# w_down as one transfer over 128 partitions in place of eight over 64, in a decode kernel that streams a KV cache

## The chip, the core and the metric

The kernel runs on one core of a Trainium2 chip. The metric is the device time of one execution in microseconds (us): 2534.58 us is the median of three runs (2534.54 to 2534.76). A separate execution was taken with the hardware profiler; it gives the page, the chain of waits, the timelines and the trace that are read below.

## The reference

One token passes through two branches that are mixed by a gate:

```python
x = A_x                                          # 1 x 1 x 512
g = sigmoid((x * gate_w).sum(-1, keepdims=True))
q = (x @ wq) as 32 heads of 128
p = softmax(q . k_cache * 128 ** -0.5)           # 32 heads x 65536 keys
a = (p @ v_cache as 4096 columns) @ wo           # 4096 x 512
b = (silu(x @ w_gate) * (x @ w_up)) @ w_down     # 512 x 1792, 512 x 1792, 1792 x 512
out = g * a + (1 - g) * b
```

All inputs are bf16. The two caches have 32 x 65536 x 128 elements each and are read once. w_down is 1792 x 512, that is 1,835,008 bytes.

## The kernel before, in words

**Tiles.** A K or a V tile is 16384 rows of one head's cache: 128 partitions with 128 rows of 128 elements each, 32 KB in a partition, 4096 KB in all. There are G = 4 tiles to a head and N = 128 tiles of each kind. All of them live in one ring of five buffers (`SLOTS`, tag "big"). wq, the pair w_gate and w_up (`gu_t`), w_down (`wd_t`) and half of wo (`wo_t`) take a turn in that ring too. So a load can start only when the tile that had its buffer five allocations earlier has been read for the last time. In order, the ring holds wq, K 0, K 1, `gu_t`, `wd_t`, and then K 2 in wq's buffer, K 3 in K 0's, K 4 in K 1's, V 0 in `gu_t`'s and K 5 in `wd_t`'s.

**Work on a tile.** VectorE (DVE) multiplies a K tile by the query (L240) and halves its columns three times by additions (L244). TensorE (PE) adds up the remaining 16 columns with identity matmuls into the scores (L254). After four K tiles the softmax of a head is made (L266 to L281). A V tile takes 32 matmuls of 128x512 (L302) with the probabilities as weights.

**Order.** The order is written out by hand: `steps` (L344 to L352) pairs each K tile with a V tile that runs several tiles behind, and the loop at L355 issues, for each step, first the loads and then the work. Every load but one is issued by SyncE (SP), in program order, so a load that waits holds back all later loads. Transfers share eight completion semaphores in turn: one waits for an earlier one to land before its semaphore is used again. These waits stand at SP's instructions in the trace.

**The small branch.** `feed_forward_in` (L169) makes x @ w_gate and x @ w_up behind K tile 1. `feed_forward_mid` (L189) forms the hidden vector `hT` on VectorE, as 128 partitions by 14 columns; two matmuls with every second column of the identity (L202) spread it over 64 partitions by 28 columns, ScalarE (ACT) copies it to `h2` (L206), and 28 matmuls of 64 rows (L209) multiply it with w_down into `b_ps`. `feed_forward_out` (L218) scales it and adds it into the output's sum `a_ps` (L227).

**w_down's load.** It lies on partitions 0 to 63, 28 rows of 512 in each, 28,672 contiguous bytes per partition. `load_wd` (L142) makes one transfer of eight partitions at a time: parts 0 and 1 at L150, ahead of K tile 2, and parts 2 to 7 at L359, behind it.

**The end.** The last V tiles come in pieces (L365), then the second half of wo in five pieces (L367). After the last V matmul stand 16 projections (L406 to L410), the copy at L413 and the store at L414.

Of the kernel before, what the change touches and what calls it, by code (L numbers as in the profile page):

```python
# [8 lines left out]
ACT = mybir.ActivationFunctionType  # L9
ALU = mybir.AluOpType  # L10
AXIS = mybir.AxisListType
P = 128
# [13 lines left out]
def kernel(  # L26
# [14 lines left out]
    nc = tc.nc  # L41
    bf16 = mybir.dt.bfloat16
    f32 = mybir.dt.float32

    _, H, Sk, Dh = A_k_cache.shape
    D = A_x.shape[2]
    F = B_w_gate.shape[1]
    KT = D // P
    FT = F // P
# [7 lines left out]
    consts = ctx.enter_context(tc.tile_pool(name="consts", bufs=1))  # L57
# [7 lines left out]
    psum_m = ctx.enter_context(tc.tile_pool(name="psum_m", bufs=2, space=bass.MemoryType.PSUM))  # L65
# [3 lines left out]
    def big(name):  # L69
        return ring.tile([P, NB * Dh], bf16, name=name, tag="big")  # L70
# [12 lines left out]
    ident_b = consts.tile([P, P], bf16, name="ident_b")  # L83
# [18 lines left out]
    def load(dst, cache, n, name, cuts=(0, NB)):  # L102
        h, g = divmod(n, G)
        t = big(name)
        view = t.rearrange("p (j d) -> p j d", d=Dh)
        src = cache[0, h, g * NB * P : (g + 1) * NB * P, :].rearrange("(p j) d -> p j d", j=NB)
        for a, b in zip(cuts[:-1], cuts[1:]):
            nc.sync.dma_start(out=view[:, a:b, :], in_=src[:, a:b, :])
        dst[n] = view
# [24 lines left out]
    nc.sync.dma_start(out=wgu_sb[:, 0], in_=B_w_gate.rearrange("(p t) f -> p t f", t=KT))  # L134
    nc.sync.dma_start(out=wgu_sb[:, 1], in_=B_w_up.rearrange("(p t) f -> p t f", t=KT))
    wd_t = big("wd_t")
    HP = P // 2
    GT = F // HP
    wd_sb = wd_t[:HP, : GT * D].rearrange("p (t n) -> p t n", t=GT)
    wd_rows = B_w_down.rearrange("(p t) n -> p t n", t=GT)  # L140

    def load_wd(*which):  # L142
        for i in which:
            lo = (0, 1, 2, 3, 32, 33, 34, 35)[i]
            part = slice(lo, lo + 29, 4)
            nc.sync.dma_start(out=wd_sb[part], in_=wd_rows[part])

    with nc.allow_non_contiguous_dma(reason="small"):
        nc.sync.dma_start(out=gwT, in_=gate_w.rearrange("(p t) -> p t", t=KT))
    load_wd(0, 1)  # L150
    WG = 4
    wo_tiles = {}

# [3 lines left out]
    def load_wo_end(cuts):  # L157
        t = big("wo_t")[:, : (H - WH) * D].rearrange("p (h n) -> p h n", n=D)
        rows = A_wo[WH * P :, :].rearrange("(h p) n -> p h n", p=P)
        for a, b in zip(cuts[:-1], cuts[1:]):  # L160
            nc.sync.dma_start(out=t[:, a:b, :], in_=rows[:, a:b, :])
        wo_end.append(t)

    def load_wo(g):
        wo_tiles[g] = wo_pool.tile([P, WG, D], bf16, name="wo_sb")
        rows = A_wo[g * WG * P : (g + 1) * WG * P, :]
        nc.sync.dma_start(out=wo_tiles[g], in_=rows.rearrange("(h p) n -> p h n", p=P))
# [21 lines left out]
    def feed_forward_mid(gu_sb, eg):  # L189
        nc.vector.tensor_scalar_add(eg, eg, 1.0)  # L190
        nc.vector.reciprocal(eg, eg)
        hprod = consts.tile([P, FT], f32, name="hprod")
        nc.vector.tensor_tensor(out=hprod, in0=gu_sb[:, :FT], in1=eg, op=ALU.mult)
        hT = consts.tile([P, FT], bf16, name="hT")
        nc.vector.tensor_tensor(out=hT, in0=hprod, in1=gu_sb[:, FT:], op=ALU.mult)
        xg = consts.tile([P, KT], f32, name="xg")
        nc.vector.tensor_tensor(out=xg, in0=xT, in1=gwT, op=ALU.mult)
        xs = consts.tile([P, 1], f32, name="xs")
        nc.vector.tensor_reduce(out=xs, in_=xg, axis=AXIS.X, op=ALU.add)
        h_ps = psum_m.tile([HP, GT], f32, name="h_ps", tag="misc")  # L200
        for r in range(2):
            nc.tensor.matmul(  # L202
                h_ps[:, r * FT : (r + 1) * FT], lhsT=ident_b[:, r::2], rhs=hT, start=True, stop=True
            )
        h2 = consts.tile([HP, GT], bf16, name="h2")
        nc.scalar.activation(out=h2, in_=h_ps, func=ACT.Copy)  # L206
        b_ps = psum_m.tile([1, D], f32, name="b_ps", tag="misc")
        for t in range(GT):
            nc.tensor.matmul(  # L209
                b_ps, lhsT=h2[:, t : t + 1], rhs=wd_sb[:, t, :], start=(t == 0), stop=(t == GT - 1)  # L210
            )
        g_ps = psum_m.tile([P, 1], f32, name="g_ps", tag="misc")
        nc.tensor.matmul(g_ps, lhsT=ones_f, rhs=xs, start=True, stop=True)
        eg2 = consts.tile([P, 1], f32, name="eg2")
        nc.scalar.activation(out=eg2, in_=g_ps, func=ACT.Exp, scale=-1.0)
        return b_ps, eg2
# [13 lines left out]
    def products(n, a=0, b=NB):  # L230

        h = n // G
        K = K_tiles[n][:, a:b, :]
        qb = q_bc[:, h * Dh : (h + 1) * Dh]
        q_rep = bass.AP(
            tensor=qb.tensor,
            offset=qb.offset,
            ap=[list(qb.ap[0]), [0, b - a], [1, Dh]],
        )
        yield nc.vector.tensor_tensor(out=K, in0=K, in1=q_rep, op=ALU.mult)  # L240
        half = Dh
        while half > WIDTH:
            half //= 2
            yield nc.vector.tensor_tensor(  # L244
                out=K[:, :, 0:half], in0=K[:, :, 0:half], in1=K[:, :, half : 2 * half],
                op=ALU.add,
            )
# [15 lines left out]
    def row_max(h):  # L263

        m = small.tile([P, 1], f32, name="m")
        nc.vector.tensor_reduce(out=m, in_=S_tiles[h], axis=AXIS.X, op=ALU.max)  # L266
        diag = small.tile([P, P], f32, name="diag")
        nc.scalar.activation(out=diag, in_=ident_f, func=ACT.Copy, scale=m)  # L268
        mT_ps = psum_m.tile([P, P], f32, name="mT_ps", tag="misc")
        nc.tensor.matmul(mT_ps, lhsT=ones_f, rhs=diag, start=True, stop=True)  # L270
        return mT_ps

    def exponentials(h, mT_ps):
        top = small.tile([P, 1], f32, name="top")
        nc.vector.tensor_reduce(out=top, in_=mT_ps, axis=AXIS.X, op=ALU.max)  # L275
        bias = small.tile([P, 1], f32, name="bias")
        nc.scalar.activation(out=bias, in_=top, func=ACT.Copy, scale=-scale)
        P_tiles[h] = ppool.tile([P, NBH], bf16, name="P_sb")
        nc.scalar.activation(  # L279
            out=P_tiles[h], in_=S_tiles[h], func=ACT.Exp, bias=bias, scale=scale,  # L280
            accum_out=rowsum[:, h : h + 1],  # L281
        )
        del S_tiles[h]
# [71 lines left out]
    for n, v in steps:  # L355
        if n is not None and n > 1:
            load(K_tiles, A_k_cache, n, "K_t")
        if n == 2:
            load_wd(2, 3, 4, 5, 6, 7)  # L359
        if n == 3:  # L360
            load_wo(0)
        if v is not None:
            if v % (WG * G) == 2 * G and v // (WG * G) + 1 < WH // WG:
                load_wo(v // (WG * G) + 1)
            load(V_tiles, A_v_cache, v, "V_t", (0, NB) if v < N - 2 else (0, 64, NB) if v < N - 1 else (0, 32, 64, 96, 112, NB))  # L365
            if v == N - 1:
                load_wo_end((0, 4, 8, 12, 14, 16))  # L367
        if n == 2:
            ff = feed_forward_mid(*ff)
        halves = (0, NB // 2)  # L370
        vector = iter(()) if n is None else products(n)
        if n == 0:
            vector = (i for a in halves for i in products(n, a, a + NB // 2))
        top_of = None
        if n is None:
            top_of = H - 1 if S_tiles else None
        elif n % G == 0 and n > 0:
            top_of = n // G - 1
            vector = (i for a in halves for i in products(n, a, a + NB // 2))
        if top_of is not None:  # L380
            next(vector, None)
            mT_ps = row_max(top_of)
            next(vector, None)
            exponentials(top_of, mT_ps)
        for _ in vector:
            pass
        if n == 1:
            ff = feed_forward_in()
        if n == 3:
            feed_forward_out(*ff)  # L390
        if tot_ps is not None:
            weight(*tot_ps)
            tot_ps = None
        if done is not None:
            head_column(done, head_copy(done))
        if v is not None:
            values(v)
        if top_of is not None:
            tot_ps = top_of, total(top_of)
        if n is not None:  # L400
            scores(n)
        if done is not None and done < WH:
            project(done)
        done = v // G if v is not None and v % G == G - 1 else None
# [40 lines left out]
```

## Time and profile before

| what | value | where |
|---|---|---|
| median of the runs shown | 2534.58 us | times |
| the profiled execution, its own time | 2534.51 us | times |
| its span | 2532.6 us | page |
| bytes read | 1087.64 MB, 429 GB/s over the span | page, part 3 |
| DMA in the main queue | 99.7% of 16 engines' span | page, part 3 |
| VectorE busy | 2175.5 us (86%) | page, part 1 |
| TensorE busy | 1742.4 us (69%) | page, part 1 |
| matmuls on w_down, 28 | 12.1 us busy, 629 ns each | page, part 5 |
| mean granted TensorE clock | 0.749 | page, cores |

The span goes from the first instruction to the last; 1.9 us of the execution's own time lie around it. The page gives each engine's busy time, a cut of the span into 40 slices, the DMA queues, the chain of waits that ended last, and the costliest groups of instructions. "<-" names what ended an engine's idle time. Beside these views the trace keeps every packet that a DMA engine moved, with its queue, start, duration and size, and a 4-byte record for each engine's completion of a transfer. It doesn't name the engine of a packet.

### The profile page before, as it was taken

The page shows a single profiled execution, that of the slowest core. Times are in us where ns is not written, and L with a number is a line of the kernel's source. Part 1 is how long each engine was busy: PE and PEld are TensorE (multiplying, and loading weights), DVE is VectorE, ACT ScalarE, POOL GpSimd, SP SyncE. Part 2 cuts the span into 40 slices and gives each one's busy share as a digit, 9 for nine tenths or more (in the row PEclk, how much of TensorE's full clock was granted, in tenths as well). Part 3 has the DMA queues.
Part 4 walks back from the last instruction along what each step waited for, and adds up shares of the span by engine and source line. Part 5 has one row for each costly group of instructions (what it writes and reads, how often), then busy time and mean ns, then how long its engine had stood idle before and what let it go on. Part 6 is the DMA issues. An engine that isn't in the chain of part 4 may idle for free.

```text
span 2532.6 us, 15260 instructions
## 1 busy us (share of the span) xinstructions
PE 1742.4 (69%) x6738; PEld 712.1 (28%) x6738; DVE 2175.5 (86%) x784; ACT 75.9 (3%) x207; POOL 0.7 (0%) x6
## 2 busy tenths in 40 slices
PE   4677666776677666676776677667666776677679
PEld 2222222222222222222222223222222232222223
DVE  7998888888888999998888888888888888888860
ACT  1000000000000000000000000000000000000000
POOL 0000000000000000000000000000000000000000
PEclk7677777777777676677777777777777777777779
DMA  9999999999999999999999999999999999999998
GB/s 415 433 433 430 433 433 433 432 430 435 432 432 434 431 433 432 432 433 433 432 434 433 432 434 433 432 432 434 432 431 434 433 430 434 434 431 433 434 432 339
DMA packets 42884, 1088.63 MB, mean 430 GB/s; under 512 B 4737, under 2 KB 8834, under 8 KB 9090
## 3 DMA queue, kind: packets, MB, share of 16 engines
q1 hardware_dynamic: 42674, 1087.66, 99.7%
q8 instruction: 53, 0.87, 0.1%
q14 instruction: 13, 0.11, 0.0%
q10 hardware_dynamic: 144, 0.00, 0.0%
HBM read 1087.64 MB, written 0.00 MB: 429 GB/s over the span
## 4 chain that ended last, share of the span: by engine, by line
DMA 68%; PE 22%; DVE 10%; issue 1%; ACT 0%; DVEq 0%; SPq 0%
DMA V_t<-in_A_v_cache_dram 61%; PE O_ps L302 20%; DMA K_t<-in_A_k_cache_dram 5%; DVE K_t L240 5%; DVE K_t L244 5%; PE S_ps L254 1%; DMA wo_t<-in_A_wo_dram 1%; DMA wq_t<-in_A_wq_dram 0%; PE qg_ps L117 0%; DVE m L266 0%; PE oh_ps L323 0%; PE a_ps L335 0%; PE a_ps L227 0%; ACT P_sb L279 0%; DVE top L275 0%
## 5 line engine op out<-in xcount | busy, mean ns | idle before, releaser
L302 PE MATMUL O_ps<-V_t,P_sb 128*4 128x512 bf16 x4096 | 1157.3, 453 | 496.8 <-DMA V_t<-in_A_v_cache_dram 494.3
L240 DVE TENSOR_TENSOR K_t<-K_t,q_bc 128x16384 bf16<-128x16384 bf16 (+1 forms) x160 | 1117.2, 6983 | 254.4 <-DMA K_t<-in_A_k_cache_dram 232.9
L244 DVE TENSOR_TENSOR K_t<-K_t 128x4096 bf16<-128x4096 bf16 (+3 forms) x480 | 1030.9, 2148 | 14.3
L302 PEld LDWEIGHTS <-P_sb 128*4 128x4 bf16 x4096 | 393.9, 97 | 1241.0 <-issue 897.5
L254 PE MATMUL S_ps<-K_t,ident_b 128*128 128x128 bf16 x2048 | 466.0, 394 | 107.0 <-DVE K_t L244 106.9
L254 PEld LDWEIGHTS <-ident_b 128*128 128x128 bf16 x2048 | 227.6, 115 | 330.0 <-issue 140.2
L323 PE MATMUL oh_ps<-ident_f,O_sb 4*128 4x1 f32 x256 | 57.9, 343 | 74.1 <-ACT O_sb L315 74.1
L323 PEld LDWEIGHTS oh_ps<-ident_f,O_sb 4*128 4x128 f32 x256 | 55.2, 314 | 83.7 <-ACT O_sb L315 78.9
L270 PE MATMUL mT_ps<-diag,ones_f 128*128 128x128 f32 x64 | 23.6, 468 | 79.8 <-ACT diag L268 79.8
L268 ACT ACTIVATE diag<-ident_f,m 128x128 f32<-128x128 f32 x32 | 12.8, 401 | 2099.3 <-DVE m L266 2099.3
L317 DVE COPY O_sb<-O_ps 4x256 f32<-4x256 f32 x1 | 0.4, 414 | 52.1 <-ACT O_sb L315 52.1
L270 PEld LDWEIGHTS mT_ps<-diag,ones_f 128*128 128x128 f32 x64 | 14.7, 285 | 95.6 <-ACT diag L268 95.6
L266 DVE TENSOR_REDUCE m<-S_ps 128x1 f32<-128x512 f32 x32 | 21.9, 683 | 7.4 <-PE S_ps L254 7.4
L315 ACT ACTIVATE O_sb<-O_ps 4x512 f32<-4x512 f32 (+1 forms) x32 | 18.1, 566 | 131.0 <-PE O_ps L302 131.0
L279 ACT ACTIVATE P_sb<-S_ps,bias 128x512 bf16<-128x512 f32 x32 | 22.0, 687 | 1.0
L117 PE MATMUL qg_ps<-wq_t,X_bc 128*128 128x512 bf16 x32 | 8.6, 436 | 13.2 <-DMA wq_t<-in_A_wq_dram 13.2
L293 DVE RECIPROCAL recip<-tot_ps 128x1 f32<-128x1 f32 x32 | 5.1, 160 | 12.2 <-PE tot_ps L288 12.2
L209 PE MATMUL b_ps<-wd_t,h 64*1 64x512 bf16 x28 | 12.1, 629 | 4.3 <-DMA K_t<-in_A_k_cache_dram 4.3
L288 PEld LDWEIGHTS tot_ps<-rowsum,ones_f 128*128 128x128 f32 x64 | 9.5, 188 | 14.0 <-issue 14.0
L288 PE MATMUL tot_ps<-rowsum,ones_f 128*128 128x1 f32 x64 | 12.2, 260 | 0.0
L330 ACT ACTIVATE oT<-oh_ps,rg 128x1 bf16<-128x1 f32 x32 | 8.4, 263 | 76.6 <-PE oh_ps L323 76.6
L227 PE MATMUL a_ps<-b_sb,ones_f 1*1 1x512 f32 x2 | 1.9, 1032 | 12.1 <-ACT b_sb L226 12.1
(42 smaller groups left out, 73.8 us busy)
## 6 DMA issues: line engine op xcount, KB each, us to landing
K_t<-in_A_k_cache_dram SPq DMA_DIRECT2D x127, 4096.0 KB, 35.3
V_t<-in_A_v_cache_dram SPq DMA_DIRECT2D x126, 4096.0 KB, 29.1
wq_t<-in_A_wq_dram SPq DMA_DIRECT2D x1, 4096.0 KB
K_t<-in_A_k_cache_dram SPq DMA_DIRECT2D x2, 2048.0 KB, 16.8
V_t<-in_A_v_cache_dram SPq DMA_DIRECT2D x2, 2048.0 KB
V_t<-in_A_v_cache_dram SPq DMA_DIRECT2D x3, 1024.0 KB, 29.4
wo_sb<-in_A_wo_dram SPq DMA_DIRECT2D x4, 512.0 KB, 17.3
gu_t<-in_B_w_gate_dram SPq DMA_DIRECT2D x1, 1792.0 KB
```

The costliest lines, as they stand in the source:

```text
L209: nc.tensor.matmul(b_ps, lhsT=h2[:, t : t + 1], rhs=wd_sb[:, t, :], start=(t == 0), stop=(t == GT - 1))
L240: yield nc.vector.tensor_tensor(out=K, in0=K, in1=q_rep, op=ALU.mult)
L244: yield nc.vector.tensor_tensor(out=K[:, :, 0:half], in0=K[:, :, 0:half], in1=K[:, :, half : 2 * half], op=ALU.add,)
L254: nc.tensor.matmul(S_tiles[h][:, g * NB : (g + 1) * NB], lhsT=ident_b, rhs=K_tiles[n][:, :, c], start=(c == 0), stop=(c == WIDTH - 1),)
L266: nc.vector.tensor_reduce(out=m, in_=S_tiles[h], axis=AXIS.X, op=ALU.max)
L268: nc.scalar.activation(out=diag, in_=ident_f, func=ACT.Copy, scale=m)
L270: nc.tensor.matmul(mT_ps, lhsT=ones_f, rhs=diag, start=True, stop=True)
L279: nc.scalar.activation(out=P_tiles[h], in_=S_tiles[h], func=ACT.Exp, bias=bias, scale=scale, accum_out=rowsum[:, h : h + 1],)
L288: nc.tensor.matmul(tot_ps, lhsT=ones_f, rhs=rowsum[:, h : h + 1], start=True, stop=True)
L302: nc.tensor.matmul(O_tiles[h], lhsT=P_tiles[h][:, g * NB + j : g * NB + j + 4], rhs=V_tiles[n][:, j : j + 4, :], start=(g == 0 and j == 0) ...
L315: nc.scalar.activation(out=O_sb[:, :cut], in_=O_ps[:, :cut], func=ACT.Copy)
L323: nc.tensor.matmul(oh_ps, lhsT=O_sb[:, c * Dh : (c + 1) * Dh], rhs=ident_f[0:4, c : c + 1], start=(c == 0), stop=(c == 3),)
```

## The change

w_down is laid out over 128 partitions, 14 rows of 512 each (14,336 contiguous bytes per partition), and loaded by one transfer that is issued behind K tile 2. The two transfers ahead of K tile 2 are gone, and so are the two spreading matmuls, their accumulator `h_ps` and ScalarE's copy to `h2`: the 14 columns of `hT` are the weights directly. 28 matmuls of 64 rows become 14 of 128 rows.

```diff
     wd_t = big("wd_t")
-    HP = P // 2
-    GT = F // HP
-    wd_sb = wd_t[:HP, : GT * D].rearrange("p (t n) -> p t n", t=GT)
-    wd_rows = B_w_down.rearrange("(p t) n -> p t n", t=GT)
-
-    def load_wd(*which):
-        for i in which:
-            lo = (0, 1, 2, 3, 32, 33, 34, 35)[i]
-            part = slice(lo, lo + 29, 4)
-            nc.sync.dma_start(out=wd_sb[part], in_=wd_rows[part])
+    wd_sb = wd_t[:, : FT * D].rearrange("p (t n) -> p t n", t=FT)
...
-    load_wd(0, 1)
...
-        h_ps = psum_m.tile([HP, GT], f32, name="h_ps", tag="misc")
-        for r in range(2):
-            nc.tensor.matmul(
-                h_ps[:, r * FT : (r + 1) * FT], lhsT=ident_b[:, r::2], rhs=hT, start=True, stop=True
-            )
-        h2 = consts.tile([HP, GT], bf16, name="h2")
-        nc.scalar.activation(out=h2, in_=h_ps, func=ACT.Copy)
         b_ps = psum_m.tile([1, D], f32, name="b_ps", tag="misc")
-        for t in range(GT):
+        for ft in range(FT):
             nc.tensor.matmul(
-                b_ps, lhsT=h2[:, t : t + 1], rhs=wd_sb[:, t, :], start=(t == 0), stop=(t == GT - 1)
+                b_ps,
+                lhsT=hT[:, ft : ft + 1],
+                rhs=wd_sb[:, ft, :],
+                start=(ft == 0),
+                stop=(ft == FT - 1),
             )
...
         if n == 2:
-            load_wd(2, 3, 4, 5, 6, 7)
+            nc.sync.dma_start(out=wd_sb, in_=B_w_down.rearrange("(p t) n -> p t n", t=FT))
```

## The prediction on record

> **What bounds the kernel.** I read the page's parts 2 and 3 first, then the chain of waits at the end, then the end's timeline. Parts 2 and 3:
>
> ```profile
> GB/s 415 433 433 430 433 433 433 432 430 435 432 432 434 431 433 432 432 433 433 432 434 433 432 434 433 432 432 434 432 431 434 433 430 434 434 431 433 434 432 339
> ...
> q1 hardware_dynamic: 42674, 1087.66, 99.7%
> q8 instruction: 53, 0.87, 0.1%
> ```
>
> The rate is flat at 430 to 435 GB/s from the second slice to the last but one, and packets occupy 99.7% of sixteen engines' time: the DMA engines bound the kernel from beginning to end, and no compute stage does. The chain at the end says what follows the last loads:
>
> ```profile
> 2472.70 31.39 DMA V_t<-in_A_v_cache_dram
> ...
> 2504.16 20.87 DMA wo_t<-in_A_wo_dram
> ...
> 2527.07 2.69 PE a_ps L335 x12
> ```
>
> and the timeline there:
>
> ```profile
> 2504.14 20.88 PE L302 MATMUL O_ps<-V_t,P_sb 128*4 128x512 bf16 x96 [1.62 <-DMA V_t<-in_A_v_cache_dram]
> ...
> 2529.79 0.68 DVE L413 CAST out_sb<-a_ps 1x512 bf16<-1x512 f32 x1 [3.85 <-PE a_ps L335]
> 2530.49 0.28 SPq L414 DMA_DIRECT2D out_dram<-out_sb  x1
> ```
>
> The 126th V tile (V 125) was issued at 2472.70 and landed at 2504.09. PE had run dry 1.62 us before, then ran 96 matmuls back to back (217 ns each), the projections and the store. So the end is V 125's landing plus 28.5 us. A transfer has landed when the last of its sixteen engines is done, so the question is **which engine is last, and what it carries**.
>
> **Sixteen engines, one by one.** The page's DMA share is a mean and hides this; I followed the trace's packets instead. 32,512 packets are 32 KB, of 1,213 ns at the 5th and the 95th percentile; the next one on an engine starts 3 ns before the end of the last. A K or V tile is eight of them per engine. w_down is 64 packets of 28,672 B (1,062 ns), and the count of completion records, 4,465, is 275 transfers x 16, plus 8 x 8, plus one for the store: **each w_down transfer ran on eight engines only**. They are the same eight each time: K tile 3, the first behind all of w_down, finishes on eight engines at 59.8 to 60.2 us and on the other eight at 68.1 to 69.5 us. The mean distance is 8.59 us, against 8 x (1,062 + 3) ns = 8.52 us. I call them the loaded and the free eight. Since no engine of the loaded eight idles after that, their lag lasts.
>
> A second load is uneven: the 53 instruction packets of 16 KB (the q8 row). After each one, one engine's completions come 1.42 us later and stay so. Packet n and n + 8 hit the same engine, so eight engines take six or seven each; two of them are loaded, six free. Followed to K tile 126, the completions are:
>
> ```
> engines                       K 126 done at, us
> loaded, with instructions x2  2416.60  2415.52
> loaded, without           x6  2406.7 to 2412.7
> free, with instructions   x6  2406.8 to 2408.5
> free, without             x2  about 2398 to 2400
> ```
>
> The last, 2416.60, plus three tiles of 9.68 us is 2445.64; the view shows the third tile behind as landed at 2446.02, and the same 0.38 us lies between record and landing at V 125. So I follow the right engine: it holds the 229 KB of w_down and seven instruction packets.
>
> **The change, part by part.** *The bytes.* All sixteen engines now take eight packets of 14,336 B. That size is in the trace, as w_gate and w_up: 535 ns, start to start 532. Eight are 4.26 us. The loaded engines lose 8.52 - 4.26 = 4.26 us, the free ones gain 4.26 us. The last engine goes from 2416.60 to 2412.34. The free ones with instructions go to 2411.1 to 2412.8; three of them get a seventh instruction packet (1.42 us) before V 125: the worst of these is 2407.16 + 1.42 + 4.26 = 2412.84. That is the new last engine, and the gain is 2416.60 - 2412.84 = **3.76 us**.
>
> *Transfers.* Seven issues fewer. On SP the six at L146 take 20.11 us, waiting for completion semaphores, and K 3 goes out at 43.20 behind them:
>
> ```profile
> 21.86 0.34 SPq L108 DMA_DIRECT2D K_t<-in_A_k_cache_dram  x1
> 22.98 20.11 SPq L146 DMA_DIRECT2D wd_t<-in_B_w_down_dram  x6
> 43.20 0.37 SPq L108 DMA_DIRECT2D K_t<-in_A_k_cache_dram  x1
> ```
>
> Afterwards K 3 waits for K 0's scores (done at 39.2) and is issued some 4 us earlier. That is worth nothing: the engines have K 2 to move until 50 us, so the queue is full either way. Taking two parts from ahead of K 2 opens no gap: K 2 is issued at 21.86, and w_up occupies the engines until about 40.8. If that cover were gone, the gap would be the wait for K 2's issue.
>
> On an engine, the next packet starts within 10 ns of a completion record, so a transfer that ends leaves no gap in a full queue. The Trainium skill, "DMA: Bandwidth & Descriptors", section "Anatomy of one DMA", gives a transfer a fixed cost of about 2 us, mostly the receipt of its last byte; seven fewer would be 14 us, and the time 2520.6 us. With the row instead of the rule the seven transfers are worth nothing, since a receipt lies beside the next transfer's packets.
>
> *Matmuls.* The 28 take 12.1 us, start to start 0.43 us, at half clock:
>
> ```profile
> 54.01 8.69 DVE L240 TENSOR_TENSOR K_t<-K_t,q_bc 128x16384 bf16<-128x16384 bf16 x1 [0.80 <-DMA K_t<-in_A_k_cache_dram]
> ...
> 60.35 12.10 PE L209 MATMUL b_ps<-wd_t,h 64*1 64x512 bf16 x28 [4.28 <-DMA K_t<-in_A_k_cache_dram]
> ```
>
> 14 of the same width take 6.0 us if 128 rows cost what 64 do (L302 has 128 rows and 0.43 us from start to start, too). With L202 (0.27 us) and the copy L206 (0.19 us) PE saves some 6.5 us here. It frees w_down's buffer for K 5, issued at 72.48, about 10 us sooner: 6.5 us of matmuls plus some 4 us of w_down's earlier landing. The queue holds K 4 and V 0 then, so the engines don't see it. VectorE's wait of 0.80 us for K 2 shrinks or goes; VectorE waits 232.9 us for K tiles over the span, so that comes back as a later wait. Cost of this part: zero; below zero only if the DMA queue were empty here, where it is not; above zero only if a full-height matmul were slower, and then by PE time that no one waits for.
>
> *The end.* PE starts on V 125 at its landing and has 1.62 us in hand there; K 127 lands earlier by nearly as much, so PE's backlog moves along. The pieces behind V 125 have 0.1 to 2 us in hand and move with the same engines. The last piece of wo landed at 2529.11, just as its matmul began, on the same last engine: it comes 4 us sooner.
>
> **Sum.** 2534.51 - 3.76 = 2530.75 us for the profiled execution, which is 0.07 us under the median of 2534.58. I forecast **2530.8 us**. Limits of this term: 4.26 us at most, if the free engines stay below (2530.3), and 2.4 us if one of them meets two of the delays of 0.6 to 1.4 us that the trace shows on single engines here and there (2532.2).
>
> **A rule that speaks against the change.** In the trace no engine is slower per packet: 1,213 ns at both percentiles. The Trainium skill, same page, section "Latency and other measured facts", says that engines 7 and 15 are usually slower in traces, though it puts this down to software-made descriptors. A slow engine among the free eight would carry 4.26 us more, and the sum would be 2538.8 us.
>
> **Rivals.**
> 1. *A free engine is last sooner than I think* (11%): same mechanism, gain 1.8 to 2.9 us, 2531.7 to 2532.7 us. For it: six free engines are within 0.5 us of the new end, and the last of several is later than each. Against: in my table the worst is already taken.
> 2. *Hidden* (4%): PE's tail of 28.5 us, or SP's late issues of wo's pieces, doesn't move with V 125. Then 2534.6 us. For it: PE is busy without a break there. Against: the 1.62 us before it.
> 3. *The wrong half* (4%): the engine that ends last is of the free eight; then 4.26 us are added: 2538.8 us. It decides from the point where a free engine ends behind the loaded ones; my table puts the nearest 8 us ahead of the last.
> 4. *Slower, by PE's clock* (6%): outside the tail the granted clock keeps falling to 0.5, where a 128x512 matmul starts every 0.43 us instead of 0.217. Were it 0.5 over the tail's 112 such matmuls, they would take 24 us more: about 2554.6 us. A single stretch of 10 us costs 5 us (2536), so it is slower by more than 0.2% from two stretches on, and it is that which I give 6%. It decides when PE idles in the tail long enough to lose full clock. Against: full clock from 2467 to past 2525, with the gap of 1.62 us in it, and runs within 0.22 us of each other.
> 5. *More than 5.07 us gained* (5%): some wait goes that I don't see. Against: the engines have no idle time to give back beyond w_down's share.
>
> **Chances and range.** Forecast (2529.9 to 2531.7) 70%. 0.2%, about what a measurement of this kernel can tell from no change, is 5.07 us: rivals 1, 2 and 3 and the forecast lie inside, 89%; rival 5 is faster, 5%; rival 4 slower, 6%. The range takes the forecast and rival 1: 2529.9 to 2532.7.
>
> **What would show it.** Completion records 4,465 - 64 + 16 = 4,417; no 28,672-B packets; K 3's sixteen completions within 2 us instead of 9; V 125 landing at 2500.3; PE's tail from there unchanged at 28.5 us to the store; w_down's 14 matmuls at about 6 us. I am wrong if K 3's completions close up and V 125 still lands near 2504, or if V 125 is early and PE's tail is longer.

## The result, and the profile after

The changed kernel takes **2540.81 us** (median of 10 runs, 2540.60 to 2541.03) against 2534.56 us of the kernel before (10 runs beside it, 2533.17 to 2536.28): 1.0026 times as long, with a 95% interval from 1.0017 to 1.0035. That is 6.25 us slower, where the prediction had 3.8 us faster. The profiled execution took 2540.70 us; its span is 2538.9 us, and its granted TensorE clock 0.752 against 0.749. The kernel before has runs near 2533.3 and runs near 2534.6 us, so its median moves by up to 1.1 us from one set of runs to another (2533.46 to 2534.56).

Parts 2 and 3 of the page of the changed kernel:

```profile
GB/s 416 430 429 429 432 432 432 430 430 430 432 432 432 429 430 431 432 432 430 431 431 433 431 429 432 433 430 429 433 433 430 431 431 431 431 432 430 432 433 356
...
q1 hardware_dynamic: 42690, 1087.66, 99.8%
q8 instruction: 52, 0.85, 0.1%
```

The engines are still full (99.8%) and move the same 1087.66 MB. But the rate is lower in nearly every slice, not in one: the mean of slices 3 to 38 is 431.0 GB/s, and it was 432.6 in the kernel before. 0.36% of the 2,300 us between is 8 us. A loss spread evenly over the whole span can't come from a wait at w_down, which is over after 62 us.

The chain that ended last, its tail:

```profile
2479.21 30.83 DMA V_t<-in_A_v_cache_dram
2510.05 0.02 issue
...
2510.11 21.09 DMA wo_t<-in_A_wo_dram
...
2533.24 2.87 PE a_ps L322 x12
```

V 125 lands at 2510.05, 5.96 us later than before. From there to the end of the span are 28.85 us, and they were 28.51: the tail hardly moved, and what was lost was lost in the stream of transfers ahead of it. SP's queue at the change, from the timeline of the changed kernel:

```profile
8.43 0.33 SPq L108 DMA_DIRECT2D K_t<-in_A_k_cache_dram  x1
21.91 0.33 SPq L346 DMA_DIRECT2D wd_t<-in_B_w_down_dram  x1
39.35 0.33 SPq L108 DMA_DIRECT2D K_t<-in_A_k_cache_dram  x1
```

w_down is one issue in place of eight. K 2 now goes out at 8.43, since its load is written first and takes the ring's fifth buffer, which is still free; w_down takes wq's. K 3's completion records lie between 63.9 and about 66 us, where they were 9.7 us apart. So the part of the change that the prediction was about did happen.

The trace's packets show what else happened. Below the two kernels stand those of the experiments that moved the ring or what lies behind it; "ring begins at" is the byte of a partition at which the ring's first buffer begins in the compiled program; the traces keep no addresses. Each median is from its own set of runs.

```
kernel                      ring begins at   32 KB packets           instruction  median
                                             of 1,213 ns  mean, ns   packets, ns  us
before                      30,976           32,361       1214.4      929         2534.56
changed                     30,912            2,070       1218.1     1066         2540.81
changed, ring moved (h1)    30,976           32,374       1214.2      928         2530.56
changed, ring moved (h5)    31,232           32,388       1214.2      927         2530.56
changed, ring moved (i2)    31,040            2,041       1218.1     1067         2540.86
changed, rest moved (i1)    30,912            3,353       1217.9     1065         2539.92
before, ring moved (h2)     31,168            2,470       1218.4     1066         2545.07
before, ring moved (h3)     31,104            7,854       1218.3     1066         2544.48
```

There are 32,512 packets of 32 KB in each. Before, 99.5% of them took 1,213 ns exactly; in the changed kernel 6%, and the usual values are 1,215 ns (16,522 packets) and 1,222 ns (6,502). From one tile to the next an engine needs 9,711 to 9,718 ns where it needed 9,681.

### The profile page after: what moved, and what is told of

Same layout as the page of the kernel before. It is cut to its first block, busy times and chain, and to the rows that moved or that the text cites. A ratio compares the mean times of both kernels' runs of the same rounds, so it can differ in the third digit from the quotient of the medians.

```text
span 2538.9 us, 15215 instructions
## 1 busy us (share of the span) xinstructions
PE 1733.3 (68%) x6722; PEld 708.3 (28%) x6722; DVE 2175.4 (86%) x784; ACT 75.7 (3%) x206; POOL 0.7 (0%) x6
## 3 DMA queue, kind: packets, MB, share of 16 engines
q1 hardware_dynamic: 42690, 1087.66, 99.8%
## 4 chain that ended last, share of the span: by engine, by line
DMA 68%; PE 22%; DVE 10%; issue 1%; ACT 0%; DVEq 0%; SPq 0%
DMA V_t<-in_A_v_cache_dram 62%; PE O_ps L289 20%; DVE K_t L227 5%; DVE K_t L231 4%; DMA K_t<-in_A_k_cache_dram 4%; PE S_ps L241 1%; DMA wo_t<-in_A_wo_dram 1%; DMA wq_t<-in_A_wq_dram 0%; PE oh_ps L310 0%; PE qg_ps L117 0%; DVE m L253 0%; PE a_ps L322 0%; ACT P_sb L266 0%; PE a_ps L214 0%; DVE top L262 0%
## 5 line engine op out<-in xcount | busy, mean ns | idle before, releaser
L262 DVE TENSOR_REDUCE top<-mT_ps 128x1 f32<-128x128 f32 x32 | 9.0, 282 | 1.0 <-PE mT_ps L257 1.0
```

## The experiments

Four explanations for the longer packets were tried. **Order**: K 2 goes out early, beside more descriptors, and sits in another buffer. **Step**: with w_down balanced the sixteen engines run in step, and collide. **Program**: PE's program is shorter, which moves its instruction packets (52 instead of 53). **Address**: a tile that the change removes moved the ring. The last one came up only when the others had failed.

### Order: e1, e6, e2

`e1_old_layout_k2_early` is the kernel before with all eight parts of w_down behind K 2, so that K 2 takes the free buffer (issued at 8.37).

```diff
-    load_wd(0, 1)
...
-            load_wd(2, 3, 4, 5, 6, 7)
+            load_wd(0, 1, 2, 3, 4, 5, 6, 7)
```

> The kernel before, with all eight w_down transfers of 64 partitions behind K tile 2 instead of two ahead of it. K tile 2 then takes the free ring buffer and is issued at about 8.4 us, as in the changed kernel, while the eight loaded engines keep their lag of 8.5 us behind the others. Theory S (in step): packets grow from 1,213 to 1,215-1,222 ns because all sixteen engines now work at the same descriptors at the same time; here half of them lag, so packets stay at 1,213 ns and the time is that of before, 2534.6 us. Rival Q (early issue): the early K tile 2, which puts 72 descriptors instead of 65 on an engine's queue at once, brings the engines into the longer packets; then packets are 1,215-1,222 ns here too, and with w_down still on eight engines the time is about 2543 us or more.

Measured: 2533.85 us (2533.39 to 2534.97) against 2533.46 in the same rounds, ratio 1.000 (0.9991 to 1.0010). `e6_k2_late` does the reverse: in the changed kernel one column of w_down's tile is written when the tile is made, so that w_down has the fifth buffer and K 2 goes out at 22.18.

```diff
     wd_t = big("wd_t")
+    nc.vector.memset(wd_t[:, 0:1], 0.0)
```

> The changed kernel with one added VectorE memset of one column of w_down's buffer at its allocation, so that w_down keeps the fifth ring buffer as in before, and K tile 2 takes wq's and is issued at about 21.9 us; w_down's single transfer follows it at about 22.3 us. Engines carry equal bytes and run in step. Theory S (in step): packets 1,215-1,222 ns, about 2540.8 us. Rival Q (early issue): the queue never holds more than 63 descriptors, packets stay at 1,213 ns, about 2530.8 us, which was the forecast for the change.

Measured: 2540.91 us, 1.0026 (1.0016 to 1.0036), packets at 1,218.1 ns. `e2_one_load_ahead_of_k2` issues the one transfer ahead of K 2:

```diff
+    nc.sync.dma_start(out=wd_sb, in_=B_w_down.rearrange("(p t) n -> p t n", t=FT))
...
-        if n == 2:
-            nc.sync.dma_start(out=wd_sb, in_=B_w_down.rearrange("(p t) n -> p t n", t=FT))
```

> The changed kernel with its single w_down transfer ahead of K tile 2 instead of behind it: w_down is issued at about 8.4 us, K tile 2 waits for the queries until 21.9 us as in before; sixteen engines carry the same bytes. Theory S (in step): longer packets as in the changed kernel, about 2540.8 us. Rival Q (early issue): an engine's queue holds the same 72 descriptors at 8.4 us, so about 2540.8 us too. A third, B (the swap of ring buffers between K tile 2 and w_down): 1,213 ns and about 2530.8 us.

Measured: 2540.86 us, 1.0026 (1.0016 to 1.0036). Neither the order of the two loads nor the buffers they sit in has to do with it: early K 2 is free in the old layout, and late K 2 brings nothing back in the new one.

### Step: e3

`e3_half_the_skew` was to bring back half of the lag between the two groups of eight engines, by giving eight transfers of eight partitions to one of them.

```diff
-            nc.sync.dma_start(out=wd_sb, in_=B_w_down.rearrange("(p t) n -> p t n", t=FT))
+            wd_rows = B_w_down.rearrange("(p t) n -> p t n", t=FT)
+            nc.sync.dma_start(out=wd_sb[0:64], in_=wd_rows[0:64])
+            for i in range(64, 72):
+                nc.sync.dma_start(out=wd_sb[i::8], in_=wd_rows[i::8])
```

> The changed kernel's layout and matmuls (128 rows), but w_down comes in nine transfers behind K tile 2: one of 64 partitions on all engines and eight of 8 partitions on eight engines only. The eight loaded engines lag by 8 x 0.535 = 4.3 us, half of before's. K tile 2 is issued early as in the changed kernel. Theory S (in step): a lag of 4.3 us, three and a half packets, is enough to part the engines; packets 1,213 ns, and the time 2534.6 - 2.1 = about 2532.5 us. Rival Q (early issue): 1,215-1,222 ns, about 2542 us. If the matmuls of 128 rows cost anything, it shows here as a time above 2532.5 us with packets of 1,213 ns.

Measured: 2550.48 us, 1.0065 (1.0050 to 1.0080). This says nothing on the question, because the lag that it was to make didn't come about: K 3's completions lie within 2.0 us, in two groups of eight 1.35 us apart in the mean, where 4.3 us were expected. Something else did. Busy time, clock, DMA share and rate by stretches, first of e3, then of the changed kernel:

```profile
52.00:64.00 12.00, 3.63 (x16) 1.82 (x15) 10.85 (x9) 0.00 (x0) 0.00 (x0) 0.50 0.85 169
```

```profile
52.00:64.00 12.00, 9.17 (x32) 3.64 (x32) 11.83 (x9) 0.17 (x1) 0.00 (x0) 0.64 1.00 431
```

The last two figures are DMA's busy share and GB/s: packets in flight for 85% of the time moved 169 GB/s. (431 - 169) x 12 us is 3.1 MB, or 7.3 us at 431 GB/s, most of the 9.7 us that this kernel lost to the changed one. The first eight 32 KB packets of K 3, which started beside these transfers at about 60 us, took 3,049 to 3,351 ns, and w_down's 128 packets 1,092 ns in the mean instead of 540. These small transfers are expensive; why, is open. They differ from those of the kernel before in two ways: they go to partitions 64 to 127 instead of 0 to 63, and each takes every eighth partition (64, 72, ... 120) instead of every fourth (0, 4, ... 28). No run separates the two. The theory of step fell another way: around 800 us the completions come in groups of seven or eight engines within 0.7 us both in the changed kernel and in the same kernel with its ring moved (h1, below), and only the first has the long packets.

### Program: f1, f2

`f1_changed_padded_pe` gives the changed kernel 16 idle matmuls, so that PE's program is as long as before. `f2_before_short_pe` takes 16 of the 28 matmuls of w_down out of the kernel before.

```diff
+        for _ in range(16):
+            nc.tensor.matmul(g_ps, lhsT=ident_b, rhs=xT[:, 0:1], start=True, stop=True)
```

```diff
-        for t in range(GT):
+        for t in range(12):
...
```

> The changed kernel with 16 idle matmuls (128x1, onto g_ps, overwritten by the real one) added in the small branch, so that PE's program has the 12,800 rows of the kernel before instead of 12,768. Engines run in step, loads as in the changed kernel. Theory S (in step): packets 1,215-1,222 ns, 2540.8 us. Theory P (program): the packets' length depends on the program's length in memory and not on the engines' lag: 53 instruction packets again, packets 1,213 ns, and the balance of bytes then gives its gain: about 2530.8 us, 2.7 us or more under before.

> The kernel before with 12 of the 28 matmuls on w_down, which leaves 16/28 of the product with w_down out of the sum, so that PE's program has the changed kernel's 12,768 rows. All loads are as before, eight engines lag by 8.5 us. Theory S (in step): the lag parts the engines, packets 1,213 ns, about 2534 us. Theory P (program): 52 instruction packets, packets 1,215-1,222 ns, and the lag of 8.5 us in full: about 2541 + 4 = 2545 us.

Measured: f1 2541.0 us, 1.0028 (1.0017 to 1.0038); it still has 52 instruction packets, so the 53 of its expectation didn't come about, and it shows only that the added PE instructions bring nothing back. f2 settles it: 2534.55 us, 0.9998 (0.9989 to 1.0008), with 52 instruction packets like the changed kernel, and its 32 KB packets at 1,213 ns. Neither PE's shorter program nor the missing 53rd instruction packet has a part in it.

### Address: h1, h5, h2, h3

What is left that could reach every transfer for 2,500 us? Their destination. The pool `consts` (L57) lies ahead of the ring in each partition. The change removes one tile from it: `h2`, 28 columns of two bytes, which takes 64 bytes. With it the ring begins at byte 30,976, which is 121 x 256. Without it, it begins at 30,912, 192 past a multiple of 256, and so do all five buffers, a whole number of 32 KB apart. `h1_changed_ring_at_30976` is the changed kernel with 64 unused bytes in `consts`:

```diff
+    pad = consts.tile([P, 16], f32, name="pad")
+    nc.vector.memset(pad[:, 0:1], 0.0)
     gval = consts.tile([P, 1], f32, name="gval")
```

> The changed kernel with a 64-byte tile added to the constants pool (and a VectorE memset of its first column), nothing else. The pool lies ahead of the ring; without the 56 bytes of h2 the ring's five buffers begin 64 bytes lower in each partition, at byte 30,912 instead of 30,976, which is no multiple of 256; the added tile puts them back at 30,976 = 121 x 256. Every kernel so far with the ring at 30,976 (before, e1, f2) has packets of 1,213 ns, every one with it at 30,912 (the changed kernel, e2, e3, e6, f1) packets of 1,213 to 1,225 ns. Theory A (address): packets back at 1,213 ns, 53 or 52 instruction packets at about 880-970 ns, and the balance of bytes gives the forecast: about 2530.8 us. Rival S (engines in step make packets longer): the loads are those of the changed kernel, so 1,215-1,222 ns and 2540.8 us.

Measured: **2530.56 us** (2530.30 to 2530.67, 11 runs), 0.9984 of the kernel before (0.9976 to 0.9993), and 10.25 us less than the changed kernel. Rate and tail of the chain, from its page and its trace:

```profile
GB/s 419 431 430 431 436 433 433 431 431 433 435 434 431 431 433 435 432 432 434 431 434 432 434 431 433 434 433 432 432 434 434 432 432 430 437 433 431 431 434 363
```

```profile
2469.46 31.05 DMA V_t<-in_A_v_cache_dram
...
2500.55 20.88 PE O_ps L291 x96
...
2523.27 2.69 PE a_ps L324 x12
```

The mean of slices 3 to 38 is 432.6 GB/s again. V 125 lands at 2500.51; the prediction had said 2500.3 for the change. `h5_changed_ring_at_31232` puts 320 bytes there instead of 64, for the next multiple of 256 above that (122 x 256):

```diff
+    pad = consts.tile([P, 80], f32, name="pad")
...
```

> The changed kernel with a 320-byte tile added: the ring begins at 31,232 = 61 x 512. Theory A with multiples of 256: as with 30,976, about 2530.8 us. If multiples of 512 are what counts, then it is faster than that one. Rival S: 2540.8 us.

Measured: 2530.56 us, 0.9985 (0.9976 to 0.9994), the same to a hundredth. The other direction is the kernel **before** with 192 and with 128 bytes in `consts`, `h2_before_ring_192_off` and `h3_before_ring_128_off`:

```diff
+    pad = consts.tile([P, 48], f32, name="pad")
...
```

```diff
+    pad = consts.tile([P, 32], f32, name="pad")
...
```

> The kernel before with a 192-byte tile added to the constants pool: its ring begins at 31,168, 192 bytes past a multiple of 256, as in the changed kernel. Eight engines lag as before. Theory A (address): packets of 1,215-1,222 ns and about 10 us more than before (the changed kernel stands 10 us above the forecast of 2530.8): about 2544 us. Rival S: no change, 2534 us.

> The kernel before with a 128-byte tile added: its ring begins at 31,104, 128 bytes past a multiple of 256. Theory A with multiples of 256: longer packets as at 192 off, about 2544 us. Theory A with multiples of 128: 1,213 ns and 2534 us. Rival S: 2534 us.

Measured: 2545.07 us, 1.0042 (1.0028 to 1.0055), and 2544.48 us, 1.0039 (1.0025 to 1.0053): some 10 us slower, without any part of the change in them. Part 2 of the page of the first:

```profile
GB/s 414 431 431 429 431 431 431 431 428 433 432 430 432 428 432 431 432 431 430 431 433 429 432 433 429 432 431 431 432 431 431 431 431 430 431 432 430 432 431 330
```

It averages 431.0 GB/s in slices 3 to 38, like the changed kernel, though it differs from the kernel before only in the address (and in one column written at the start).

### How far the address carries: i1, i2

In `i1_ring_off_rest_back` the ring stays at 30,912, and a 64-byte pool between the ring and the pools behind it puts those back to where they lie in the kernel before. It has the same additional tile and the same write as h1.

```diff
     ring = ctx.enter_context(tc.tile_pool(name="ring", bufs=SLOTS))
+    gap = ctx.enter_context(tc.tile_pool(name="gap", bufs=1))
...
+    pad = gap.tile([P, 16], f32, name="pad")
+    nc.vector.memset(pad[:, 0:1], 0.0)
```

> The changed kernel; the ring stays at byte 30,912 of each partition (192 past a multiple of 256), but a 64-byte tile in a pool of its own between the ring and the pool of small tiles puts everything behind the ring back to the byte it has before the change. If the ring's own address is what costs (my theory), nothing is won: 2540.8 us (2540.4 to 2541.2), 32 KB packets at a mean of about 1,218 ns, a tile's pitch of 9,711 ns on an engine. If it is the address of what lies behind the ring (the small tiles, the probabilities, wo's buffers), or the mere presence of one more small tile and its write, the time is that of the ring at 30,976: 2530.6 us, with 1,214 ns and 9,681 ns.

Measured: 2539.92 us (2539.84 to 2541.38), 1.0022 (1.0012 to 1.0032). So it is the ring's own address that costs, and not what lies behind it, nor one tile more: 9.36 of the 10.25 us remain. The other 0.9 us I didn't expect. They are there when V 125 lands, too (2509.12 against 2510.05), and 1,283 more packets take 1,213 ns. These lie in a few stretches: between 50 and 100 us 62% of the 32 KB packets take 1,213 ns, between 850 and 900 us 55%, and in most others 5 to 7%, as in the changed kernel; why, is open. `i2_changed_ring_64_off` has 128 bytes in `consts`, so that the ring begins at 31,040, 64 past a multiple of 256:

```diff
+    pad = consts.tile([P, 32], f32, name="pad")
...
```

> The changed kernel with a 128-byte tile in the pool ahead of the ring: the ring begins at byte 31,040, 64 past a multiple of 256. If every start off a multiple of 256 costs the same (my theory, since 128 off and 192 off cost 9.9 and 10.5 us on the kernel before): 2540 to 2541.5 us, 32 KB packets at 1,218 ns, pitch 9,711 ns. If the cost grows with the distance from the multiple of 256, a third of that of 192: about 2534 us, with a pitch near 9,691 ns. If 64 bytes are free: 2530.6 us.

Measured: 2540.86 us, 1.0026 (1.0017 to 1.0036). 64, 128 and 192 bytes past cost the same, about 10 us; two starts at a multiple of 256 cost nothing. The cost is a step, not a slope. Counted from where the ring lies in the kernel before: moved by 0 or 256 bytes it is fast, moved by -64, 64, 128 or 192 bytes it is slow.

VectorE, which works on the K tiles in the ring, isn't needed for it. Between 2480 and 2500 us it is idle in the changed kernel (0.00 us busy), and still only 6% of the 32 KB packets take 1,213 ns there, against all of them in h1.

The Trainium skill, "DMA: Bandwidth & Descriptors", section "How a descriptor splits into AXI transactions", has a rule that points at the same boundary: a transaction must start at a multiple of 256 B, so a descriptor (here one run of 32 KB) that starts elsewhere begins at the boundary below, and the bytes in between are fetched for nothing. The runs agree on the boundary. They don't agree on the size that follows from the page: 64, 128 and 192 unused bytes are 2, 4 and 6 beats (the page's 32 B steps) in 1,024, an estimate of 0.2%, 0.4% and 0.6% more time; measured were 0.32%, 0.33% and 0.33%, by the mean packet of i2, h3 and h2 against the same kernel with the ring at 30,976. Nor does the page speak of the written side, which is what was moved here. What the engines do in that time no run here shows.

## Why the prediction was wrong, point by point

- **DMA engines bound the kernel throughout.** Right: 99.7% before, 99.8% after, and nearly all that was lost or won is there when V 125 lands.
- **The loaded and the free eight; 3.76 us to gain.** Right, once the address is kept: h1 gains 4.0 us in medians (2534.52 - 2530.56) and V 125 lands 0.2 us from the time given. The two kernels at 192 past a multiple of 256, without the change (h2) and with it, differ by about as much: 2545.07 - 2540.81 = 4.26 us. Which engine ends last in h1 wasn't followed, so an agreement to 0.2 us may be luck in part. K 3's completions closed up to 2 us, and there are 4,417 completion records and no packet of 28,672 B.
- **Packet durations.** This is the step that failed: "of 1,213 ns at the 5th and the 95th percentile" was carried over to the changed kernel as a constant, and the removal of `h2` was priced by its copy alone ("the copy L206 (0.19 us)"). Removing the tile moved the ring, a cost that stands nowhere in the sum: 10.25 us, the changed kernel less h1. Per engine, 2,032 packets of 32 KB x 3.9 ns are 7.9 us, and 6.5 instruction packets x 138 ns 0.9 us. Of the 9.54 us between V 125's landings in the changed kernel and h1 that is 8.8; the other sizes are longer too (14,336 B by 3 ns, 8 KB by 5 ns), and the rest I didn't trace. Behind V 125 comes another 0.56 us (28.85 against 28.29); 0.27 of it is a wait of PE for wo, which h1 doesn't have.
- **Seven transfers fewer.** Worth nothing, as the prediction read from the row: h1 gains about what the bytes give, not 14 us. The section that the prediction cites for 2 us a transfer describes transfers issued by GpSimd; here SyncE issues all but one.
- **SP's queue.** I had w_down in its old place in the ring, and K 2 issued at 21.86. It went out at 8.43, in the free buffer, and w_down at 21.91. The pool hands out a buffer at a tile's first use in the program, so moving a load moves the buffers too. It was worth nothing, as e1 and e6 show. K 3 went out at 39.35, as predicted, behind K 0's scores.
- **Matmuls.** Fourteen took 5.2 us, predicted 6.0, worth nothing either way:

```profile
53.23 8.68 DVE L227 TENSOR_TENSOR K_t<-K_t,q_bc 128x16384 bf16<-128x16384 bf16 x1
...
56.58 5.23 PE L192 MATMUL b_ps<-wd_t,hT 128*1 128x512 bf16 x14 [0.63 <-DMA wd_t<-in_B_w_down_dram]
```

  VectorE's wait of 0.80 us for K 2 is gone, as said. PE now waits 0.63 us for w_down itself, and has time for it.
- **The rivals.** None holds. Rival 3 gave 2538.8 us, close to the time measured, but that is chance: were the free eight last, h1 would have lost 4.26 us, and it gained 4.0. Rival 4's clock didn't fall (0.752). I had written: wrong if "K 3's completions close up and V 125 still lands near 2504". They closed up, and V 125 was even later.

The prediction weighed the engines as they were, with a rule about slow engines against it, and never asked what the removed lines had allocated.

## What to carry to other kernels

Before pricing an edit that adds or removes a tile, see which buffers lie behind it in the same memory and where they begin afterwards; in a kernel bound by transfers, a large buffer 64 bytes off a multiple of 256 cost 0.4% here, more than the change could gain. Compare packet durations of one size between the two traces first: a rate that is lower in every slice points to the packets, a rate that is lower in one slice to a wait. The best version of this kernel is the change with 64 bytes of padding, at 2530.56 us.

## What the runs showed of the hardware

- Transfers from HBM into buffers at 64, 128 or 192 bytes past a multiple of 256 in the partition took 1,218 ns instead of 1,214 ns per 32 KB in the mean; the instruction packets, which don't go to the ring, grew with them, from 929 to 1,066 ns for 16 KB.
- The longer packets don't begin at once. In the changed kernel 0 of 111 packets between 14 and 18 us are longer than before, and 95 of 96 between 38 and 42 us (before: 0 of 96). wq, K 0 and K 1 had gone into the same ring by then, at the old durations. On one engine, about every third or fourth packet took 1,220 to 1,226 ns, and those between mostly 1,215 ns; over the whole run 29% of the 32 KB packets took 1,219 ns or more. Both are open.
- Eight transfers of eight partitions each, every eighth partition from 64 on, came with a rate of 169 GB/s for 12 us (e3); the kernel before made eight transfers of every fourth partition among 0 to 63 at no visible loss of rate (428 to 441 GB/s between 40 and 70 us).
